# Storing split weights at decode instead of re-splitting them, with ScalarE allowed the q and k copies and a new GpSimd cost in the planner

## The chip, the cores and the metric

One core of one Trainium2 chip runs the kernel. The metric is device time in microseconds of that core, a median of several runs. TensorE is called PE in the profile, VectorE DVE, ScalarE ACT, GpSimd POOL, SyncE SP. Every DMA of this kernel is issued from SP's queue, which is worked off in order.

## The reference, cut to what matters

```python
# q, k, v: [4, 8, 576, 64], f: [4, 8, 576]
scores = q @ k^T / 8 + cum[i] - cum[j]          # cum: running sum of log f; causal
attn = softmax(scores); x = (attn @ v) as [2304, 512]
x = ((x @ w_a) * (x @ w_b)) @ w_out              # first layer, d_ff = 1536
xn = x / rms(x) * rms_g
out = (silu(xn @ w_gate) * (xn @ w_val)) @ w_out2  # second layer
```

Weights arrive as float64 bit patterns. A weight is decoded to float32 and then split into a high part (float32r) and a low part, so that one product becomes three matmuls: high by high, high by low, low by high.

## The kernel before, in words

**Phases.** The 2304 tokens are cut into three chunks of 576, 704 and 1024 tokens. `PHASES` is a list of six (layer m, chunk c): (0,0), (0,1), (1,0), (1,1), (0,2), (1,2), called phases 0 to 5 here. In the trace phase 0 ends at about 235 us, phase 1 at 400, phase 2 at 555, phase 3 at 715. Phases 0 and 2 (`plan_plain`) multiply plainly. Phases 1, 3, 4 and 5 (`plan_wino`) use seven products in place of eight. Attention of the four batches is woven into phases 0 to 3.

**Weights.** An f-tile is 128 of the 1536 inner columns; there are 12 in a layer (FT), taken in thirds of four (QF). Each f-tile has two granules j = 2f and 2f+1 (w_a and w_b, or gate and value), and each third four granules of w_out. In phases 0 and 2 `decode` makes every granule once: SP loads `raw` (512 KB, a ring of two tiles), ACT rebases (L775), DVE shifts (L779) and joins (L783), ACT rounds to the high part (L1646), POOL subtracts for the low part (L791). The result is a `w` tile (512 KB, a ring of seven). A w_out granule is stored split (`wd`, 512 KB, L796); an input granule is stored unsplit (`wf`, 256 KB, L810).

**Re-splitting.** Phases 1 and 3 call `sums` for every f-tile. It loads both unsplit granules (L738), calls `again` for each, which splits them once more (ACT L750, DVE or POOL L753) and stores the split halves to `wd` (L824: 512 KB of the granule "one", 256 KB of "two"). Then it adds and subtracts quarters (L839, DVE or POOL), splits the two combined tiles (ACT L847, DVE or POOL L850) and stores them (`ws`). Phases 4 and 5 load `wd` and `ws` only (L1213). Phase 0 also calls `again` for granules whose second token half comes later.

**Attention.** For three batches `head` copies q twice and k twice per head, rounding them (L1922, on POOL alone), and DVE subtracts for the low parts (L1925).

**Order of the work.** The program is planned ahead: `Plan.op` records each operation with its engine or a tuple of allowed engines, a cost in ns and a priority; `Plan.run` is a list schedule that starts the operation that can start first and, for a tuple, takes the engine that would end it first; `Plan.order` tries nine priority offsets for each 30 us. The costs (`act`, `dve`, `pool1`, `pool2` and so on) are all that it knows of the chip. POOL and DVE operations marked `port` are never planned at one time. Each engine's order is then fixed, so any cost that changes can change the order everywhere.

Of the kernel before, what the change touches and what calls it, by code (L numbers as in the profile page):

```python
# [13 lines left out]
AF = mybir.ActivationFunctionType  # L14
ALU = mybir.AluOpType
# [5 lines left out]
KT, FT = DM // 128, DFF // 128  # L21
# [9 lines left out]
PE, ACT, DVE, POOL, SP = "PE", "ACT", "DVE", "POOL", "SP"  # L31
# [20 lines left out]
    (((3, ALL, 0),), ((2, 0.1, 1.0, 0.7), (3, 0.1, 0.88, 0.3)), 20000),  # L52
]
NG = 2 * FT + 3 * KT

LOADS, SEL = (0, 2, 4, 8), 4

# [38 lines left out]
def act(n, psum=False):  # L96
    return (51 if psum else 93) + n / 1.2
# [6 lines left out]
def dve2(n):  # L104
    return 67 + n / 1.92
# [4 lines left out]


def pool1(n):
    return 55 + n / 0.96


def pool2(n):
    return 75 + 2.25 * n


def half(c, s):  # L120
# [263 lines left out]
class Kernel:  # L384
# [219 lines left out]
    def blocks(self, p):  # L604

        m, c = PHASES[p]
        n = range(len(CHUNKS[c][1]))
        if c == 0:
            if p:
                return [x for q in range(THIRDS) for x in self.plain_blocks(q, n)]  # L610
            ab = lambda fs, ss: [("ab", j, s) for f in fs for j in (2 * f, 2 * f + 1) for s in ss]
            y = lambda q, ss: [("y", i, q, s) for i in range(KT) for s in ss]
            cut = QF + ALONE
            return [
                *self.plain_blocks(0, [0]), *ab(range(QF, cut), [0]), *ab(range(cut, 2 * QF), n),
                *ab(range(QF, cut), [1]), *y(1, n), *self.plain_blocks(2, n), *self.plain_blocks(0, [1]),
            ]
        ahead = int(self.adjoins(p))
        out = [*((x, f) for f in range(2) for x in ("P1", "P2")), ("P7", 0)] if ahead else [("P1", 0), ("P7", 0), ("P2", 0)]
        for f in range(FT):  # L620
            out += [("P6", f), ("P4", f)]
            nxt = [[(x, f + 1)] if f + 1 < FT and (x == "P7" or f >= ahead) else [] for x in ("P1", "P7", "P2")]
            out += [*nxt[0], ("P5", f), *nxt[1], *nxt[2], ("P3", f)]
            if f == FT - 1 or (p < SWAP_AT and f % QF == QF - 1):
                out += [("y", i, f // QF, s) for i in range(KT) for s in n]
            elif p >= SWAP_AT and f and f % QF == FAST_AFTER:
                out += [("z", i, f // QF - 1, k) for k in range(len(FAST)) for i in range(KT // 2)]
        if self.adjoins(p + 1):
            out[-2 * KT :] = [("y", i, THIRDS - 1, s) for s in n for i in range(KT)]
        return out  # L630
# [86 lines left out]
    def weights(self, m, j, t, start=0):  # L717
# [13 lines left out]
        )  # L731
        return w

    def words_of(self, m, j, prio):

        x = self.tile([128, 2, 256], "w32", W32_BUFS, I32, pool=self.dec)
        self.op(
            SP, 420, lambda *_: self.nc.sync.dma_start(self.row(x).bitcast(F32), self.wf[m][j]), reads=[("wf", m, j)],  # L738
            writes=[(x, k) for k in range(2)], prio=prio, nbytes=262144,
        )  # L740
        return x
# [17 lines left out]
    def decode(self, m, js, t, start=0):  # L759

        nc, op = self.nc, self.op
        for j in js:
# [29 lines left out]
                    out=w.tile[:, :, 1, :], in0=i32.tile.bitcast(F32), in1=w.tile[:, :, 0, :].bitcast(F32), op=ALU.subtract  # L792
                )

            def save(j=j, w=w):
                nc.sync.dma_start(self.wd[m][j], self.flat(w.tile))  # L796

            op(SP, 420, load, writes=[raw], prio=t - 14000, nbytes=524288, start=start)
            both = [(i32, k) for k in range(2)]
# [3 lines left out]
            duo = DUO if t < 0 else (ACT,)  # L803
            op(duo, (act(512), dve2(512))[: len(duo)], high, reads=both, writes=[(w, 0)], prio=t - 6000, port=True)
            op(POOL, pool2(512), low, reads=[*both, (w, 0)], writes=[(w, 1)], prio=t - 5500)
            if j >= 2 * FT:
                op(SP, 420, save, reads=[(w, 0), (w, 1)], writes=[("wd", m, j)], prio=t - 4000, nbytes=524288)
            else:
                op(
                    SP, 420, lambda *_, j=j, x=i32: nc.sync.dma_start(self.wf[m][j], self.row(x).bitcast(F32)), reads=both,  # L810
                    writes=[("wf", m, j)], prio=t - 3500, nbytes=262144,
                )
            self.fresh[m, j] = w

    def sums(self, m, f, t):
# [2 lines left out]
        js = (2 * f + 1, 2 * f) if m else (2 * f, 2 * f + 1)  # L818
        one, two = words = [self.words_of(m, j, t - 24000) for j in js]
        whole = []  # L820
        for a, (j, x) in enumerate(zip(js, words)):
            y = self.again(m, j, x, t, a, -3000)
            op(
                SP, 420, lambda y=y, j=j, o=512 * a: nc.sync.dma_start(self.wd[m][j][:, o:], self.flat(y.tile)[:, o:]),  # L824
                reads=[(y, 0), (y, 1)], writes=[("wd", m, j)], prio=t, nbytes=512 * (1024 - 512 * a),
            )
            whole.append(y)
# [357 lines left out]
    def plan_wino(self, p, m, c):  # L1185
# [12 lines left out]
        def load(kind, f, t):  # L1198
            if (kind, f) in loaded:
                return loaded[kind, f]  # L1200
            make = p in SUMS_IN
            if make:
                for x, y in zip((0, 1, "one", "two"), self.sums(m, f, t)):
                    loaded[x, f] = y
                return loaded[kind, f]
            y = self.w_tile()
            if kind in ("one", "two"):
                j = 2 * f + ((kind == "one") == (m == 1))
                key, src, cut = ("wd", m, j), self.wd[m][j], 512 if kind == "two" else 0
            else:  # L1210
                key, src, cut = ("ws", m, f, kind), self.ws[m][f][kind], 0
            op(
                SP, 420, lambda z: nc.sync.dma_start(self.flat(z)[:, cut:], src[:, cut:]),  # L1213
                reads=[key], writes=[(y, 0), (y, 1)], prio=t - 9000, nbytes=512 * (1024 - cut),
            )
            loaded[kind, f] = y
            return y
# [382 lines left out]
    def plan_boot(self):  # L1600
# [12 lines left out]
            self.first_pair(i, FIRST[i % 2], t0 + BOOT_STEP * i)  # L1613
        boot = list(self.plan.nodes)
        self.rows_out(ROWS_AT)
        self.decode(0, (0, 1), t0 + EARLY_AT, EARLY_START)
        self.swapped = self.op(None, 0, self.swap, writes=["late"], after=boot, prio=0)

    def first_loads(self, t):
# [30 lines left out]
    def first_pair(self, i, u, t):  # L1650
# [49 lines left out]
        def each(fn, eng, cost, reads, writes, dt, port=False):  # L1700
            for g in range(2):
                op(eng, cost, partial(fn, g), reads=reads(g), writes=writes(g), prio=t + dt + 100 * g, port=port)
# [9 lines left out]
            writes=both, prio=t + 1900,  # L1712
        )
        op(DVE, 76, lambda *_: nc.vector.reciprocal(out=sm.tile, in_=sm.tile), writes=both, prio=t + 2000)
        each(norm, TRIO, (act(e) + 93, dve2(e) + 62, pool2(e) + 270), of(sm), of(p), 2200, port=True)
        ps, pv = (self.bank(*x) for x in ((("s", S_BANKS) if i % 2 else ("tp", TP_BANKS),) * 2))
        each(transpose, PE, turn_cost(nkb, n), of(p), of(ps), 3500)
        m = 2 * nkb * n
# [193 lines left out]
    def head(self, g, q0, k1, t, sf, b, qk, vr, v):  # L1912
# [5 lines left out]
        if sf:  # L1918
            return [pair], own, values

        def copy(out, x):
            nc.gpsimd.tensor_scalar(out=out, in0=x, scalar1=1.0, scalar2=0.0, op0=ALU.mult, op1=ALU.add)  # L1922

        def rest(out, x, high):
            nc.vector.tensor_tensor(out=out, in0=x, in1=high.bitcast(F32), op=ALU.subtract)  # L1925
# [2 lines left out]
        q, k = (qk, g, 0), (qk, g, 1)  # L1928
        qa, ka = (self.tile([128, S], x + "a", 2, F32R, pool=self.att) for x in "qk")
        n = k1 - q0  # L1930
        op(POOL, pool1(n), lambda x: copy(x[0:64, q0:k1], qr()[:, q0:k1]), reads=[q], writes=[(qa, 0)], prio=t - 9000)
        op(POOL, pool1(n), lambda: copy(b.tile[0:64, g, 0, q0:k1], qr()[:, q0:k1]), reads=[q], writes=[(b, g, 0, 0)], prio=t - 8000)
        op(
            DVE, dve(n), lambda: rest(qa.tile[64:128, q0:k1], qr()[:, q0:k1], qa.tile[0:64, q0:k1]),
            reads=[q, (qa, 0)], writes=[(qa, 1)], prio=t - 7000, port=True,
        )
        op(POOL, pool1(k1), lambda x: copy(x[0:64, :k1], kr()[:, :k1]), reads=[k], writes=[(ka, 0)], prio=t - 7000)
        op(POOL, pool1(k1), lambda: copy(ka.tile[64:128, :k1], kr()[:, :k1]), reads=[k], writes=[(ka, 1)], prio=t - 6000)
        op(
            DVE, dve(k1), lambda: rest(b.tile[0:64, g, 1, :k1], kr()[:, :k1], ka.tile[64:128, :k1]),  # L1940
            reads=[k, (ka, 1)], writes=[(b, g, 1, 0)], prio=t - 5000, port=True,
# [214 lines left out]
```

## Time and profile before

| | |
|---|---|
| median of 3 runs | 1071.0 us (1070.7 to 1071.8) |
| profiled execution, its own time | 1069.92 us |
| its span, first to last instruction | 1068.1 us |
| PE busy | 1041.4 us (98%) |
| DVE, ACT, POOL busy | 845.6, 590.4, 277.2 us |
| moved by DMA | 217.33 MB, mean 203 GB/s |

The span is 1.8 us under the execution's own time, and the execution 1.1 us under the median. Matmuls overlap in the pipeline and their ends are modelled, so that 98% busy says that PE was seldom idle, and not that it ran at its peak.

### The profile page before, as it was taken

To read this page: it belongs to the slowest core of one execution; us is meant where nothing else is said; L and a number is where in the kernel's file an instruction comes from. 1 tells how busy PE (TensorE), PEld (TensorE's weight loads), DVE (VectorE), ACT (ScalarE), POOL (GpSimd) and SP (SyncE) were. 2 spreads that over 40 slices of the span, in tenths; PEclk is the share of its full clock that TensorE was granted. 3 is DMA by queue.
4 is the path that set the end of the run, shared out by engine and by line. 5 is a ranking of instruction groups with operands and counts; after the bars stand their busy time and mean duration, and the time that the engine had idled before them with its cause. 6 is when DMAs were issued, how large, how long until landed. Compare 5 with 4: busy or idle time off the path is not lost.

```text
span 1068.1 us, 19135 instructions
## 1 busy us (share of the span) xinstructions
PE 1041.4 (98%) x6716; PEld 932.8 (87%) x6716; DVE 845.6 (79%) x1893; ACT 590.4 (55%) x1292; POOL 277.2 (26%) x299
## 2 busy tenths in 40 slices
PE   9899999999999999999999999999999999999998
PEld 7678899899999999999989999988888887788886
DVE  7888777799498978988889688866567469979974
ACT  8787766757463766765666664613333254444330
POOL 3444455411222344536341011110000023212000
PEclk9999999999999999999999999999999999999999
DMA  7887465879476845666769576686453634546332
GB/s 195 247 264 242 145 222 169 251 249 346 146 268 210 322 143 153 207 196 215 218 233 331 192 265 258 250 285 198 140 170 123 205 120 148 173 138 182 120 122 79
DMA packets 84848, 217.33 MB, mean 203 GB/s; under 512 B 12320, under 2 KB 22768, under 8 KB 84752
## 3 DMA queue, kind: packets, MB, share of 16 engines
q1 hardware_dynamic: 84752, 216.11, 61.9%
q8 instruction: 53, 0.87, 0.3%
q14 instruction: 43, 0.35, 0.1%
HBM read 141.32 MB, written 74.74 MB: 202 GB/s over the span
## 4 chain that ended last, share of the span: by engine, by line
PE 69%; DVE 13%; DMA 7%; ACT 6%; issue 2%; POOL 2%; SPq 0%; ACTq 0%; DVEq 0%; POOLq 0%
PE m L932 16%; PE m L934 16%; PE m L933 16%; PE s L933 2%; PE s L934 2%; PE s L932 2%; PE s L1954 2%; DMA raw<-wo 2%; PE tp L933 2%; PE tp L934 2%; PE tp L932 2%; PE tp L1595 2%; DVE w L783 2%; PE tp L2018 2%; ACT P L1554 1%
## 5 line engine op out<-in xcount | busy, mean ns | idle before, releaser
L932 PE MATMUL m<-E,w 128*128 128x512 f32 (+3 forms) x672 | 232.8, 346 | 2.5 <-DVE xc L1409 1.3
L934 PE MATMUL m<-E,w 128*128 128x512 f32 (+3 forms) x672 | 228.5, 340 | 2.6 <-DVE w L850 2.3
L933 PE MATMUL m<-E,w 128*128 128x512 f32 (+3 forms) x624 | 213.5, 342 | 0.0
L1321 ACT ACTIVATE a<-m 128x352 f32<-128x352 f32 (+1 forms) x144 | 74.9, 526 | 133.0 <-PE m L934 132.3
L791 POOL TENSOR_TENSOR w<-w,w 128x512 fp32r<-128x512 f32 x72 | 99.5, 1388 | 171.9 <-ACT w L1646 150.8
L932 PEld LDWEIGHTS m<-E,w 128*128 128x128 f32 x672 | 127.3, 189 | 16.8 <-issue 1.8
L933 PE MATMUL m<-Eb,w 128*128 128x352 f32 (+3 forms) x432 | 140.9, 326 | 0.0
L934 PEld LDWEIGHTS m<-E,w 128*128 128x128 f32 x672 | 127.1, 189 | 14.1 <-DVE w L850 2.9
L932 PE MATMUL m<-Eb,w 128*128 128x352 f32 (+3 forms) x384 | 127.7, 333 | 2.0 <-DVE a L1330 2.0
L1330 DVE TENSOR_TENSOR a<-m,a 128x352 f32<-128x352 f32 (+1 forms) x144 | 86.0, 602 | 53.4 <-PE m L934 49.7
L933 PEld LDWEIGHTS m<-E,w 128*128 128x128 f32 x624 | 118.3, 190 | 10.8 <-issue 0.2
L934 PE MATMUL m<-Eb,w 128*128 128x352 f32 (+3 forms) x384 | 126.7, 330 | 0.0
L932 PE MATMUL m<-G,w 128*128 128x352 f32 (+2 forms) x352 | 111.8, 318 | 0.2 <-DVE a L1330 0.2
L933 PE MATMUL m<-G,w 128*128 128x352 f32 (+2 forms) x352 | 108.5, 308 | 1.8 <-DVE G L1460 1.8
L934 PE MATMUL m<-G,w 128*128 128x352 f32 (+2 forms) x352 | 108.4, 308 | 0.0
L1554 ACT ACTIVATE P<-P,mn 128x512 f32<-128x512 f32 (+4 forms) x128 | 76.2, 598 | 16.0 <-DVE mn L1547 15.3
L933 PEld LDWEIGHTS m<-Eb,w 128*128 128x128 f32 x432 | 81.3, 188 | 4.2
L932 PEld LDWEIGHTS m<-Eb,w 128*128 128x128 f32 x384 | 72.1, 188 | 7.9 <-DVE a L1330 2.7
L934 PEld LDWEIGHTS m<-Eb,w 128*128 128x128 f32 x384 | 72.2, 188 | 4.2
L933 PEld LDWEIGHTS m<-G,w 128*128 128x128 f32 x352 | 66.3, 188 | 2.9 <-DVE G L1460 2.2
L932 PEld LDWEIGHTS m<-G,w 128*128 128x128 f32 x352 | 66.4, 189 | 1.8 <-DVE a L1330 0.5
L1547 DVE CUSTOM_DVE_ANT_0 P<-s,mask 128x512 f32<-128x512 f32 (+4 forms) x128 | 61.6, 495 | 7.2 <-PE s L1954 4.0
(271 smaller groups left out, 2337.8 us busy)
## 6 DMA issues: line engine op xcount, KB each, us to landing
w<-wd SPq DMA_DIRECT2D x52, 512.0 KB
wd<-w SPq DMA_DIRECT2D x48, 512.0 KB
ws<-w SPq DMA_DIRECT2D x48, 512.0 KB
w<-ws SPq DMA_DIRECT2D x48, 512.0 KB
w<-wf SPq DMA_DIRECT2D x60, 256.0 KB
wf<-w SPq DMA_DIRECT2D x48, 256.0 KB
raw<-wo SPq DMA_DIRECT2D x24, 512.0 KB
G<-wd SPq DMA_DIRECT2D x18, 512.0 KB
```

The source lines that it names most:

```text
L783: nc.vector.scalar_tensor_tensor(out=x, in0=words(I32, 0), scalar=29, in1=x, op0=ALU.logical_shift_right, op1=ALU.bitwise_or)
L791: nc.gpsimd.tensor_tensor(out=w.tile[:, :, 1, :], in0=i32.tile.bitcast(F32), in1=w.tile[:, :, 0, :].bitcast(F32), op=ALU.subtract)
L932: mm_(o, wh, xh, start=start, stop=False)
L933: mm_(o, wh, xl, start=False, stop=False)
L934: mm_(o, wl, xh, start=False, stop=stop)
L1321: nc.scalar.activation(z[:, :h], bank_.tile[:, :h], AF.Copy)
L1330: nc.vector.tensor_tensor(out=z, in0=bank_.tile[:, :h], in1=z, op=ALU.add)
L1547: nc.vector.tensor_tensor_reduce(out=p.tile[:n, i * w : i * w + w], in0=s[i].tile[:n, :w], in1=masks[i][:n], scale=-0.125, scalar=mn.tile[ ...
L1554: nc.scalar.activation(o, o, AF.Exp, bias=mn.tile[:n, len(s) - 1 : len(s)], scale=-1.0, accum_out=sm.tile[:n, g : g + 1])
L1595: nc.tensor.transpose(ps.tile[:w, c : c + n], p.tile[:n, i * 128 : i * 128 + w], self.ident[:n, :n])
L1954: self.nc.tensor.matmul(x[:n, :e], q.tile[:, a:e], k.tile[:, :e], start=j == 0, stop=j == len(pairs) - 1)
L2018: nc.tensor.matmul(x[64 * g : 64 * g + 64, o : o + n], tiles[g][2][0].tile[:k, i, :], y.tile[:k, to : to + n], start=i == 0, stop=i == blo ...
```

## The change

Input granules get their split form stored when they are decoded, whole for "one" and the second half for "two", except the last third of layer 0 (`ANEW`, f-tiles 8 to 11), for which everything stays as it was. `wf` is stored as before. In `sums` the calls of `again` and the `wd` stores are left only for those four f-tiles; for the other 20 (8 of layer 0, 12 of layer 1) the tiles "one" and "two" are loaded from `wd` in phases 1 and 3, as in phases 4 and 5. Phase 0 takes the last third first and the first third last. The four q and k copies may run on ACT or POOL. The planner takes `pool1` as 80 ns and `pool2` as 30 ns longer; the norm step of the first pairs is corrected by 30 ns, so that its sum stays.

```diff
+ANEW = (FT - QF, FT)
...
 def pool1(n):
-    return 55 + n / 0.96
+    return 135 + n / 0.96
...
 def pool2(n):
-    return 75 + 2.25 * n
+    return 105 + 2.25 * n
...
-                *self.plain_blocks(0, [0]), *ab(range(QF, cut), [0]), *ab(range(cut, 2 * QF), n),
-                *ab(range(QF, cut), [1]), *y(1, n), *self.plain_blocks(2, n), *self.plain_blocks(0, [1]),
+                *self.plain_blocks(2, [0]), *ab(range(QF, cut), [0]), *ab(range(cut, 2 * QF), n),
+                *ab(range(QF, cut), [1]), *y(1, n), *self.plain_blocks(0, n), *self.plain_blocks(2, [1]),
...
+    @staticmethod
+    def anew(m, f):
+        return m == 0 and ANEW[0] <= f < ANEW[1]
...
-            def save(j=j, w=w):
-                nc.sync.dma_start(self.wd[m][j], self.flat(w.tile))
+            o = 512 * (j < 2 * FT and j % 2 != m)
+
+            def save(j=j, w=w, o=o):
+                nc.sync.dma_start(self.wd[m][j][:, o:], self.flat(w.tile)[:, o:])
...
-            if j >= 2 * FT:
-                op(SP, 420, save, reads=[(w, 0), (w, 1)], writes=[("wd", m, j)], prio=t - 4000, nbytes=524288)
-            else:
+            if j >= 2 * FT or not self.anew(m, j // 2):
+                op(SP, 420, save, reads=[(w, 0), (w, 1)], writes=[("wd", m, j)], prio=t - 4000, nbytes=512 * (1024 - o))
+            if j < 2 * FT:
                 op(
...
-        for a, (j, x) in enumerate(zip(js, words)):
+        for a, (j, x) in enumerate(zip(js, words) if self.anew(m, f) else ()):
             y = self.again(m, j, x, t, a, -3000)
...
-            if make:
+            if make and (kind in (0, 1) or self.anew(m, f)):
                 for x, y in zip((0, 1, "one", "two"), self.sums(m, f, t)):
...
-        self.decode(0, (0, 1), t0 + EARLY_AT, EARLY_START)
+        self.decode(0, (2 * (FT - QF), 2 * (FT - QF) + 1), t0 + EARLY_AT, EARLY_START)
...
-        each(norm, TRIO, (act(e) + 93, dve2(e) + 62, pool2(e) + 270), of(sm), of(p), 2200, port=True)
+        each(norm, TRIO, (act(e) + 93, dve2(e) + 62, pool2(e) + 240), of(sm), of(p), 2200, port=True)
...
-        op(POOL, pool1(n), lambda x: copy(x[0:64, q0:k1], qr()[:, q0:k1]), reads=[q], writes=[(qa, 0)], prio=t - 9000)
+        op((ACT, POOL), (act(n), pool1(n)), lambda by, x: copy(by, x[0:64, q0:k1], qr()[:, q0:k1]), reads=[q], writes=[(qa, 0)], prio=t - 9000)
```

The other three copies change in the same way; on ACT a copy is an activation of the kind Copy.

## Rows read from the trace of the kernel before

**Rows 1.** The page's head and section 1: busy us, share, instructions.

```profile
span 1068.1 us, 19135 instructions
...
PE 1041.4 (98%) x6716; PEld 932.8 (87%) x6716; DVE 845.6 (79%) x1893; ACT 590.4 (55%) x1292; POOL 277.2 (26%) x299
```

**Rows 2.** Windows by stage, with their head line.

```profile
core 0: us, PE busy (x) PEld busy (x) DVE busy (x) ACT busy (x) POOL busy (x), PEclk, DMA share, GB/s
0.00:60.00 60.00, 54.48 (x396) 41.77 (x397) 48.78 (x168) 48.90 (x127) 24.32 (x32) 0.97 0.79 217
60.00:235.00 175.00, 169.06 (x1424) 155.24 (x1422) 141.59 (x384) 124.21 (x311) 79.16 (x99) 1.00 0.71 222
235.00:400.00 165.00, 163.24 (x1135) 160.03 (x1136) 135.81 (x340) 97.27 (x228) 44.06 (x54) 1.00 0.68 239
400.00:555.00 155.00, 150.90 (x1258) 144.73 (x1257) 133.94 (x344) 103.58 (x244) 71.69 (x65) 1.00 0.67 204
555.00:715.00 160.00, 156.25 (x999) 150.02 (x998) 123.11 (x263) 86.64 (x186) 18.30 (x24) 0.99 0.71 259
715.00:1069.00 354.00, 347.50 (x1513) 281.01 (x1512) 262.38 (x399) 129.85 (x199) 39.67 (x27) 1.00 0.47 149
```

**Rows 3.** PE's waits: us in total, times, longest; four of 21 rows.

```profile
PE s L1954 <- DVE mn L1547: 2.7, 5, 1.2
PE m L934 <- DVE w L850: 2.3, 1, 2.3
...
PE m L933 <- DVE G L1460: 1.8, 2, 1.6
...
PE s L1978 <- DVE b L1925: 1.0, 2, 0.6
```

**Rows 4.** Windows, all engines: the start of phase 3.

```profile
557.50:560.10 2.60, 0.31 (x2) 0.02 (x1) 1.59 (x4) 0.97 (x3) 1.86 (x3) 1.00 0.05 16
560.80:564.20 3.40, 3.40 (x15) 3.15 (x14) 3.28 (x7) 1.87 (x4) 0.00 (x0) 0.50 0.90 287
```

**Rows 5.** Timeline of ACT there: start, us, instruction, idle before.

```profile
557.21 0.92 ACT L750 ACTIVATE w<-w 128x512 fp32r<-128x512 f32 x2
558.03 0.44 ACT L1321 ACTIVATE a<-m 128x352 f32<-128x352 f32 x1
```

**Rows 6.** Timeline of DVE there.

```profile
558.51 0.53 DVE L1330 TENSOR_TENSOR a<-m,a 128x352 f32<-128x352 f32 x1 [3.06 <-ACT a L1321]
558.95 0.58 DVE L1568 TENSOR_SCALAR sm<-sm 128x2 f32<-128x2 f32 x1
559.42 0.68 DVE L850 TENSOR_TENSOR w<-w,w 128x512 fp32r<-128x512 f32 x1
...
561.09 1.02 DVE L753 TENSOR_TENSOR w<-w,w 128x512 fp32r<-128x512 f32 x2
```

**Rows 7.** Timeline of POOL there.

```profile
551.72 0.74 POOL L839 TENSOR_TENSOR w<-w,w 128x256 f32<-128x256 f32 x1 [3.01 <-DVE w L839]
...
555.90 0.73 POOL L839 TENSOR_TENSOR w<-w 128x256 f32<-128x256 f32 x1
...
557.34 2.16 POOL L1922 TENSOR_SCALAR ka<-qk 64x576 fp32r<-64x576 f32 x3
```

**Rows 8.** Instructions of line 1568: duration ns min/median/max.

```profile
L1568 DVE TENSOR_SCALAR sm<-sm x72: 142/164/1255, 25.7 to 625.1; 128x2 f32<-128x2 f32 x56, 128x1 f32<-128x1 f32 x16
```

**Rows 9.** Timeline of DVE at the end of phase 0.

```profile
235.29 0.48 DVE L1460 TENSOR_TENSOR G<-a,G 128x320 fp32r<-128x320 f32 x1
```

**Rows 10.** Windows of line 1922 alone, 0 to 715 us: the sum.

```profile
sum 715.00, POOL 82.63; mean POOL 16.53
```

**Rows 11.** Timeline of SP: loads of one raw tile, two cycles apart.

```profile
487.46 0.33 SPq L772 DMA_DIRECT2D raw<-wo  x1
...
502.72 0.33 SPq L772 DMA_DIRECT2D raw<-wv  x1
```

**Rows 12.** Windows of line 775 alone, phase 2.

```profile
400.00:555.00 155.00, 18.84 (x28) 1.00 0.67 204
```

More of the change, by code (lines that the diff above doesn't have):

```diff
@@ L1919, in head, with copy @@
             return [pair], own, values
-        def copy(out, x):
-            nc.gpsimd.tensor_scalar(out=out, in0=x, scalar1=1.0, scalar2=0.0, op0=ALU.mult, op1=ALU.add)
+        def copy(by, out, x):
+            if by == ACT:
+                nc.scalar.activation(out, x, AF.Copy)
+            else:
+                nc.gpsimd.tensor_scalar(out=out, in0=x, scalar1=1.0, scalar2=0.0, op0=ALU.mult, op1=ALU.add)
         def rest(out, x, high):
@@ L1930, in head @@
         n = k1 - q0
-        op(POOL, pool1(n), lambda x: copy(x[0:64, q0:k1], qr()[:, q0:k1]), reads=[q], writes=[(qa, 0)], prio=t - 9000)
-        op(POOL, pool1(n), lambda: copy(b.tile[0:64, g, 0, q0:k1], qr()[:, q0:k1]), reads=[q], writes=[(b, g, 0, 0)], prio=t - 8000)
+        op((ACT, POOL), (act(n), pool1(n)), lambda by, x: copy(by, x[0:64, q0:k1], qr()[:, q0:k1]), reads=[q], writes=[(qa, 0)], prio=t - 9000)
+        op((ACT, POOL), (act(n), pool1(n)), lambda by, *_: copy(by, b.tile[0:64, g, 0, q0:k1], qr()[:, q0:k1]), reads=[q], writes=[(b, g, 0, 0)], prio=t - 8000)
         op(
@@ L1936, in head @@
         )
-        op(POOL, pool1(k1), lambda x: copy(x[0:64, :k1], kr()[:, :k1]), reads=[k], writes=[(ka, 0)], prio=t - 7000)
-        op(POOL, pool1(k1), lambda: copy(ka.tile[64:128, :k1], kr()[:, :k1]), reads=[k], writes=[(ka, 1)], prio=t - 6000)
+        op((ACT, POOL), (act(k1), pool1(k1)), lambda by, x: copy(by, x[0:64, :k1], kr()[:, :k1]), reads=[k], writes=[(ka, 0)], prio=t - 7000)
+        op((ACT, POOL), (act(k1), pool1(k1)), lambda by, *_: copy(by, ka.tile[64:128, :k1], kr()[:, :k1]), reads=[k], writes=[(ka, 1)], prio=t - 6000)
         op(
```

## The prediction

> **What bounds the kernel now.** I read the page's engine line first: PE is busy 1041.4 of 1068.1 us [rows 1]. The change removes no matmul, so it can win only what lies between those two numbers, plus what PE loses while nominally busy. Next come the windows by stage [rows 2]: PE's idle time (length less busy) is 5.5 us before 60, 5.9 to 235, 1.8 to 400, 4.1 to 555, 3.8 to 715, and 5.6 of the 353.1 us left to the end. Phases 4 and 5 are untouched, so 21.1 us of idle are in reach at the very most. The other engines are 77 to 86% (DVE) and 54 to 71% (ACT) busy in the four middle stages: busy enough that a late instruction in their fixed order is felt, not so busy that their sums bound anything. Third come PE's waits, which are many and small [rows 3]. One stands out: 2.3 us for line 850, the low half of a combined tile made by `sums`. No row of that list names a DMA, so weights arrive in time today.
>
> That wait is the start of phase 3 [rows 4]: from 557.5 to 560.1 PE works 0.31 us and DMA stands nearly still. Soon after, from 560.8 to 564.2, the granted clock is 0.50, which is 1.2 GHz in place of 2.4. Those 3.4 us do the work of 1.7. So this one hole costs about 2.3 + 1.7 = 4.0 us, the largest single piece that the change can touch.
>
> How it arises is read from three timelines. On POOL the quarter steps of `sums` begin at 551.72 and the third starts at 555.90, 4.18 us later, although one takes 0.74; the time between goes to q and k copies that stand between them in POOL's order [rows 7]. On ACT two calls of `again` for the next f-tile take 0.92 us just before line 1321 [rows 5]. On DVE line 850 stands behind line 1330, which had waited 3.06 us for that line 1321 [rows 6].
>
> **The change part by part.**
>
> *Re-splitting gone.* Of 24 f-tiles 20 lose two ACT calls (0.92 us the pair [rows 5]) and two DVE or POOL calls (1.02 us the pair [rows 6]): 18 us of ACT and 20 us of DVE in all, off PE's path except where a stage starts. At phase 3's start the pair ahead of line 1321 goes, which brings lines 1321, 1330 and 850 forward by 0.8 us (558.03 less 557.21), and a pair ahead of the first quarter step goes too, about 1.0 us by the same durations. That is 1.8 of 2.3. The quarter steps could save more, 4.18 − 2 × 0.74 = 2.7 us, if the copies between them leave POOL. Once the hole is short the slow stretch behind it should go as well. I take −4.0. Bounds: −4.0 (all) and 0 (the hole stays or moves).
>
> At the end of phase 0 PE waits 1.6 us once for line 1460 [rows 3], which runs at 235.29 on DVE [rows 9] after the first `sums` of phase 1 and the combinations of its input. A pair of 1.02 us less in front: I take −1.0, bounds −1.6 and 0.
>
> *Copies on ACT or POOL.* They are 82.6 us of POOL [rows 10]. ACT is planned as shorter, but is busier, so I let half move: 41 us more on ACT, which is busy 374 us in the four stages before 555 [rows 2], so +11%. PE's waits behind these copies are 1.0 us in the row of line 1925 [rows 3]; its waits on ACT should grow in the measure of ACT's load, which on the few us of such waits is some tenths. I take −0.5, bounds −1.2 and +0.8.
>
> One row shows what a copy does to DVE beyond its own chain: line 1568, two columns wide, takes 0.58 us at 558.95 while POOL runs three copies up to 559.50 [rows 6, 7], against a median of 0.164 and a longest of 1.255 [rows 8]. The Trainium skill (SBUF — State Buffer, "SBUF: two separate sides") says that VectorE and GpSimd share one pair of ports as an exclusive lock, held for the whole instruction, and that ScalarE has its own. By that rule each copy moved frees DVE for all of its time, and the term would be up to the 2.7 us of PE's waits on line 1547 larger, −3.2 in place of −0.5. The row agrees with the lock; it does not show that PE waited for it.
>
> *Stores at decode.* Each f-tile stores 512 + 256 KB, 0.786 MB. 8 of them in phase 0 add 6.3 MB, 12 in phase 2 add 9.4 MB; the same bytes leave phases 1 and 3. Phase 2 goes from 204 to 265 GB/s and by proportion from 0.67 to 0.87 of the DMA engines' time; phase 0 (60 to 235) from 0.71 to 0.83 [rows 2]. What is late next is `raw`: with two tiles, the next load waits for the join of the one before the last. One tile's loads at 487.46 and 502.72 are two cycles apart [rows 11], 7.6 us a cycle, 3.8 us a granule. The stage needs 28 granules in 155 us [rows 12], 5.5 us each, attention included. At 204/0.67 = 305 GB/s one further 512 KB ahead of a load costs 1.7 us, 0.86 us a granule: 4.7, still under 5.5. Where no attention is between, PE takes a granule in about the ring's own time, and there the delay counts. I count 8 stored granules in each of phases 0 and 2 so, hence the upper bound 16 × 0.86 = 13.8 us; lower bound 0. Seven `w` tiles lie between decode and PE, so I stay near the lower end, +1.5.
>
> The Trainium skill speaks against this part: DMA: Bandwidth & Descriptors, "Latency and other measured facts", gives HBM's access latency as 0.2 us on average and 2 us at high load. By it each load would take up to 1.8 us longer, and the same 16 granules would cost 16 × 0.9 = 14 us, an estimate from that page. No run here shows the latency by itself.
>
> *Loads in phases 1 and 3.* 20 f-tiles load 0.786 MB each from `wd`, 15.7 MB, as much as the stores that left. Phases 4 and 5 load the same tiles with no DMA in PE's waits. I take 0. Upper bound: one hole like phase 3's 2.35 us at each of two starts, +4.7. A gain is excluded, since nothing waits for these tiles now.
>
> *Order of thirds, early decode, longer GpSimd costs.* The blocks are the same in number and size; the last third, decoded in the crowded first 72 us, is the one that stores nothing new. 0, but the whole list is ordered anew: ±2 us, as large as the single waits that such an order makes or removes [rows 3].
>
> Sum: −4.0 − 1.0 − 0.5 + 1.5 + 0 = −4.0 us. Against the profiled execution's 1069.9 that is 1065.9; it stands 1.1 under the median, so the median goes from 1071.0 to **1067.0 us**.
>
> **The rivals.**
> *The waits move (about 1071).* The hole at phase 3's start closes, but another opens elsewhere, or the first `wd` load is late there: −4.0 − 1.0 − 0.5 + 1.5 + 4.7 = +0.7, 1071.7. For it: none of PE's 21 rows of waits comes from a shortage, all come from order. Against: ACT and DVE have 18 and 20 us less to do in the order.
> *The stores hold decode back (slower).* Place: `raw` in phase 2 and the middle of phase 0. Price: 13.8 against gains of 5.5, +8.3, 1079; with half caught by the `w` ring 13.8/2 − 5.5 = +1.4, 1072.4. It decides once each stored granule costs over 5.5/16 = 0.34 us. For it: DMA at 0.87. Against: 4.7 under 5.5.
> *A better order everywhere (faster).* The planner's GpSimd times were short; with them right and copies off POOL, half of the 5.9 and 4.1 us idle of phases 0 and 2 goes, 5 us more: 1062.
> *The change does nothing* is part of the first rival: if planner and rings absorb all, ±2.
>
> **How the numbers follow.** Forecast 0.48, with a range of its own of 1063 to 1068.8; waits move 0.20; stores bite 0.20; better order 0.12. Two measurements of this kernel are told apart from about 0.2%, 2.1 us. Faster: 0.48 + 0.12 = 0.60. Same: the waits that move, 0.20. Slower: the stores, 0.20. The range reaches from the better order, 1061, to the nearer half of the stores, 1075; outside stay about 0.05 below and 0.1 above.
>
> **What would show it.** The longest wait of PE in phase 3's start is under 1 us and no half-clock stretch follows (else the −4.0 fails). Line 750 has 20 calls, not 60; bytes moved rise from 217 to 233 MB. Phase 2 shows about 265 GB/s; a cycle of `raw` stays under 9.3 us, and PE's waits name no weight from line 791 (else the stores bite). L1922's copies show on ACT about as often as on POOL. The prediction is wrong if PE's idle time in phases 0 and 2 together grows by more than 5 us, or if phases 1 and 3 show PE waiting for DMA.

## The result, and the profile after

The kernel after takes 1058.25 us (1057.13 to 1059.58, 4 runs), the kernel before in the same comparison 1071.4. The ratio is 0.9877, 95% interval [0.986, 0.9894]: 13 us faster, three times the forecast 4, and below the range. The profiled execution took 1057.13 us, its span is 1055.4.

The page's head and engine line answer to [rows 1]. The other rows are from its sections on DMA.

```profile
span 1055.4 us, 19131 instructions
...
PE 1036.5 (98%) x6716; PEld 931.0 (88%) x6716; DVE 830.3 (79%) x1877; ACT 605.6 (57%) x1324; POOL 193.2 (18%) x203
...
DMA packets 90607, 233.05 MB, mean 221 GB/s; under 512 B 12960, under 2 KB 23408, under 8 KB 90512
...
w<-wd SPq DMA_DIRECT2D x72, 512.0 KB
...
w<-wd SPq DMA_DIRECT2D x44, 256.0 KB
```

PE does the same 6716 matmuls. Its idle time, span less busy, falls from 1068.1 − 1041.4 = 26.7 to 18.9 us, and its busy time by 4.9 us. POOL loses 84 us of work, ACT gains 15, DVE loses 15, and 15.7 MB more are moved.

For the stages I divided both kernels where PE begins the blocks of a new phase. First the windows of before, for the three phases that matter, divided so:

```profile
60.00:237.60 177.60, 170.83 (x1436) 157.01 (x1435) 144.19 (x392) 125.65 (x315) 79.16 (x99) 1.00 0.71 223
...
390.40:555.30 164.90, 160.80 (x1331) 154.45 (x1330) 142.30 (x365) 110.38 (x261) 77.61 (x74) 1.00 0.65 200
555.30:702.10 146.80, 143.05 (x940) 139.20 (x939) 117.59 (x254) 83.30 (x180) 17.25 (x22) 0.99 0.69 253
```

And the windows of after, columns as in [rows 2]:

```profile
0.00:60.00 60.00, 54.76 (x414) 42.04 (x415) 50.04 (x173) 48.97 (x126) 20.83 (x28) 0.97 0.77 217
60.00:233.20 173.20, 168.26 (x1417) 156.22 (x1416) 145.13 (x392) 140.59 (x353) 53.53 (x58) 1.00 0.81 263
233.20:383.00 149.80, 148.99 (x1017) 145.84 (x1016) 115.52 (x285) 83.50 (x193) 28.43 (x35) 1.00 0.73 254
383.00:549.50 166.50, 164.07 (x1370) 157.49 (x1370) 140.98 (x375) 126.56 (x293) 64.44 (x60) 1.00 0.79 260
549.50:690.70 141.20, 140.05 (x940) 137.66 (x939) 109.15 (x232) 72.88 (x158) 11.69 (x14) 1.00 0.73 259
690.70:1056.00 365.30, 360.33 (x1570) 291.70 (x1568) 269.52 (x424) 133.13 (x204) 14.24 (x11) 1.00 0.48 155
```

PE's idle time, length less busy, falls by 6.8 − 4.9 = 1.8 us in phase 0, by 4.1 − 2.4 = 1.7 in phase 2 and by 3.8 − 1.2 = 2.6 in phase 3. Phase 3's part was forecast; phases 0 and 2, where the copies and the decoding are, were not. The DMA shares of 0.81 and 0.79 at 263 and 260 GB/s are those that the prediction worked out (0.83 and 0.87 at 265), a little lower.

PE's waits after, nine of 19 rows, the longest first, columns as in [rows 3]:

```profile
PE tp L1603 <- ACT P L1586: 2.1, 3, 1.1
PE s L1965 <- DVE mn L1555: 2.0, 5, 0.7
PE tp L1603 <- ACT w L781: 1.6, 1, 1.6
PE m L940 <- ACT a L1329: 1.2, 2, 0.7
PE tp L2029 <- ACT pt L2076: 1.2, 3, 0.5
PE warm L1616 <- DVE ones L430: 1.1, 1, 1.1
PE tp L1603 <- ACT pt L2076: 0.9, 3, 0.4
PE m L940 <- DMA w<-wd: 0.6, 2, 0.4
...
PE m L942 <- POOL w L797: 0.5, 1, 0.5
```

Lines 850 and 1460, the 2.3 and 1.8 us of [rows 3], have left the list (they are 858 and 1468 here). The list sums to 14.6 us against 22.2 in 21 rows before; the waits on DVE alone fall from 17.2 to 5.1, those on ACT rise from 4.5 to 7.9. The last two rows shown are new: waits for a stored tile at the start of phase 1 and for a decoded low half (L797, which is L791 before).

The windows at phase 3's start answer to [rows 4]:

```profile
549.50:552.10 2.60, 2.60 (x19) 2.60 (x18) 2.57 (x6) 2.38 (x6) 1.17 (x2) 1.00 1.05 409
552.10:555.50 3.40, 3.40 (x23) 3.40 (x22) 3.15 (x7) 1.97 (x5) 0.74 (x1) 1.00 1.03 385
```

PE works without a gap and keeps its full clock, where before it worked 0.31 of 2.60 us and then ran at 0.50 for 3.4 us [rows 4].

Last, the line of `again` and the windows of the copies alone (up to 691 us, ACT's line and then POOL's):

```profile
L756 ACT ACTIVATE w<-w x20: 407/618/635, 111.9 to 348.4; 128x512 fp32r<-128x512 f32 x16, 128x256 fp32r<-128x256 f32 x4
```

```profile
0.00:691.00 691.00, 37.17 (x70) 1.00 0.77 256
```

```profile
0.00:691.00 691.00, 35.91 (x58) 1.00 0.77 256
```

`again` runs 20 times, and 70 of the 128 copies went to ACT, about half, both as predicted.

### The profile page after: what moved, and what is told of

Same layout as the page of the kernel before. It is cut to its first block, busy times and chain, and to the rows that moved or that the text cites. A ratio compares the mean times of both kernels' runs of the same rounds, so it can differ in the third digit from the quotient of the medians.

```text
span 1055.4 us, 19131 instructions
## 1 busy us (share of the span) xinstructions
PE 1036.5 (98%) x6716; PEld 931.0 (88%) x6716; DVE 830.3 (79%) x1877; ACT 605.6 (57%) x1324; POOL 193.2 (18%) x203
## 4 chain that ended last, share of the span: by engine, by line
PE 62%; DVE 13%; ACT 9%; DMA 8%; issue 6%; POOL 2%; SPq 0%; DVEq 0%; POOLq 0%; ACTq 0%
PE m L940 15%; PE m L942 14%; PE m L941 14%; PE s L941 2%; PE s L942 2%; PE s L940 2%; ACT P L1562 2%; PE tp L941 2%; PE tp L942 2%; PE tp L940 2%; DMA raw<-wv 2%; DVE w L789 2%; DMA w<-wd 1%; PE tp L2029 1%; PE tp L1603 1%
## 5 line engine op out<-in xcount | busy, mean ns | idle before, releaser
L797 POOL TENSOR_TENSOR w<-w,w 128x512 fp32r<-128x512 f32 x72 | 97.1, 1354 | 201.7 <-ACT w L1654 161.3
L941 PEld LDWEIGHTS m<-E,w 128*128 128x128 f32 x624 | 118.2, 189 | 10.8
L1465 ACT ACTIVATE G<-a 128x352 fp32r<-128x352 f32 (+3 forms) x100 | 47.1, 473 | 46.1 <-DVE a L1451 17.8
L940 PEld LDWEIGHTS m<-G,w 128*128 128x128 f32 x352 | 66.2, 188 | 2.9 <-issue 1.7
```

What stands on the lines that cost most here:

```text
L797: nc.gpsimd.tensor_tensor(out=w.tile[:, :, 1, :], in0=i32.tile.bitcast(F32), in1=w.tile[:, :, 0, :].bitcast(F32), op=ALU.subtract)
L940: mm_(o, wh, xh, start=start, stop=False)
L941: mm_(o, wh, xl, start=False, stop=False)
L1465: nc.scalar.activation(out(0), x(), AF.Copy)
```

## The experiments

Two theories stood at first. By the first the gain is the re-splitting that went: its two holes were most of the forecast. By the second it is the copies that left POOL. A third came up at once: the planner writes every order anew, so a part may win or lose only because its list came out well.

**One part at a time, and the order shaken without any part.** Each is the kernel before with one part of the diff; the fourth changes one planner cost by 1 ns, so that only the order differs.

```diff
 e1_stores_alone: the lines of decode, sums and the order of thirds, nothing else
 e2_copies_alone: the four copies on (ACT, POOL), nothing else
 e3_costs_alone: pool1 55 -> 135, pool2 75 -> 105, norm 270 -> 240
 e4_order_shaken:
-    return 69 + n / 0.96
+    return 70 + n / 0.96
```

> The kernel before with the stores at decode and the order of thirds alone; q and k copies on GpSimd only, GpSimd costs as before. Theory A (re-splitting gone is the gain): at least 8 of the 13 us, 1063 or less, with phases 1 and 3 shorter. Theory B (copies or the GpSimd costs are the gain): within 3 us of before, 1068 to 1073, or slower where the stores delay the raw loads. Theory C (any new order of the list gives some us either way): anything between 1063 and 1076.

> The kernel before with the q and k copies allowed on ScalarE or GpSimd, nothing else. Theory A: within 3 us of before. Theory B, copies: phases 0 to 3 lose the waits behind GpSimd, 1064 or less, and the hole of 2.3 us at the start of phase 3 closes although both calls of the second split are still there. Theory C: 1066 to 1076, with no relation to what was moved.

> The kernel before with the planner's longer GpSimd times alone; the same operations on the same engines or nearly so. Theory A: within 3 us of before. Theory B, costs: 1066 or less, since waits on GpSimd that the plan did not foresee go. Theory C: 1066 to 1076.

> The kernel before with one cost of the planner 1 ns longer (VectorE's fixed part, 70 in place of 69 ns), so the work is the same and only its order may differ. Theory C (a new order is worth some us by itself): moves by over 3 us, up or down. Theories A and B: within 2 us of before.

Measured: stores alone 0.9945 [0.9925, 0.9966], copies alone 0.9871 [0.9846, 0.9896], costs alone 0.9956 [0.9939, 0.9973], order shaken 0.9974 [0.9958, 0.9991]. The copies alone give as much as the whole change, 13 us or more. But the costs, which take no work away and only reorder it, with 27 of POOL's 299 instructions put on DVE and ACT, "give" 4.7, and a shaken order 2.8, so no single ratio can be read to better than some 0.4%.

**One part left out, and the orders of both shaken.** The next runs take one part out of the change, or shake the orders of the copies, of the change and once more of before (69 to 71).

```diff
 e5_without_copies: the change, all four copies on POOL
 e6_without_stores: the change, without the new stores, with `again` for all f-tiles
 e14_stores_and_copies: the change, pool1, pool2 and norm as before
 e7_copies_shaken (copies alone), e13_change_shaken (the change):
-    return 69 + n / 0.96
+    return 70 + n / 0.96
 e18_order_shaken_again (the kernel before):
-    return 69 + n / 0.96
+    return 71 + n / 0.96
```

> The changed kernel with the q and k copies put back on GpSimd alone: stores and GpSimd costs stay. Theory B (the copies off GpSimd carry the change): most of the gain is gone, 0.993 to 0.998 of before. Theory A (stores and costs carry it together): 0.990 or less. Theory C (each new order is some us by luck): no better than a guess, 0.985 to 1.000.

> The changed kernel with the stores and the order of thirds taken back: copies on ScalarE or GpSimd and the longer GpSimd costs alone. Theory B: as good as the whole change or as the copies alone, 0.985 to 0.990. Theory A (the stores give some us more): 0.991 or more. Theory C: 0.985 to 1.000.

> The changed kernel with the planner's old GpSimd costs. With copies on either engine every kernel so far stands at 0.987 to 0.994; if the costs are worth nothing of their own, this one stands there too, and the stores' part cannot be told from the scatter of orders. If the costs are needed with the stores, 0.995 or more.

> The copies alone on the kernel before, with one VectorE cost of the planner 1 ns longer. Theory B: 0.985 to 0.990, as the copies alone in the first order. Theory C (that 0.987 was a lucky order): falls back to 0.993 or more.

> The changed kernel with one VectorE cost of the planner 1 ns longer. If the change's 0.988 is what its parts are worth, 0.985 to 0.991. If it is a lucky order, it goes to the level of the copies shaken, 0.991 to 0.995.

> The kernel before with DVE's planner cost 69 made 71, nothing else. If the kernels with all q and k copies on GpSimd scatter as those measured so far (0.9945 to 1.0018, mean 0.998), it lies there again, 1066 to 1074 us. If a gain of over 0.7% can come from an order alone, without copies, it can lie below 0.993.

Together with the first runs this makes 13 kernels with the same rings. The table has the ratio to before; the mean clock of TensorE over the runs; the mean time multiplied by that clock, which is an estimate of what the kernel would take had no stretch run at half clock (before was measured in five comparisons: its mean times lie from 1071.5 to 1073.1 us, this product only from 1065.5 to 1066.2); and from the one profiled execution of each PE's idle time (span less busy) and the sum of PE's waits on DVE over the rows of its list.

| copies | kernel | ratio, 95% interval | clock | time × clock, us | PE idle, us | waits on DVE, us |
|---|---|---|---|---|---|---|
| POOL | before (95 runs) | 1 | 0.9939 | 1065.9 | 26.7 | 17.2 |
| POOL | e1 stores | 0.9945 [0.9925, 0.9966] | 0.9949 | 1062.0 | 24.6 | 13.5 |
| POOL | e3 costs | 0.9956 [0.9939, 0.9973] | 0.9939 | 1061.9 | 26.0 | 14.2 |
| POOL | e4 shaken | 0.9974 [0.9958, 0.9991] | 0.9954 | 1065.3 | 25.4 | 15.1 |
| POOL | e5 stores, costs | 1.0018 [0.9998, 1.0038] | 0.9917 | 1064.2 | 25.1 | 15.9 |
| POOL | e18 shaken | 0.9971 [0.9941, 1.0] | 0.9929 | 1061.9 | 23.4 | 10.8 |
| either | after | 0.9877 [0.986, 0.9894] | 0.9983 | 1056.5 | 18.9 | 5.1 |
| either | e2 copies | 0.9871 [0.9846, 0.9896] | 0.9950 | 1054.1 | 17.1 | 8.2 |
| either | e6 copies, costs | 0.9941 [0.9913, 0.9969] | 0.9946 | 1057.9 | 20.1 | 9.3 |
| either | e7 copies, shaken | 0.9929 [0.9906, 0.9953] | 0.9968 | 1058.8 | 20.7 | 10.0 |
| ACT | e12 copies | 0.9941 [0.9923, 0.9958] | 0.9934 | 1058.7 | 20.7 | 10.7 |
| either | e13 all, shaken | 0.9938 [0.9911, 0.9964] | 0.9946 | 1058.5 | 20.3 | 8.5 |
| either | e14 stores, copies | 0.9950 [0.9932, 0.9967] | 0.9954 | 1061.5 | 21.1 | 9.6 |

With the copies on POOL alone the means of the last three columns are 1063.5, 25.2 and 14.5 us; with the copies movable they are 1058.0, 19.8 and 8.8. No kernel of one group reaches into the other: 1061.5 stands against 1061.9, 21.1 against 23.4, 10.7 against 10.8. So movable copies are worth about 5.5 us of work (standard error 1.1 from the scatter in the groups), and it shows as 5.4 us less idle time of PE and as 5.7 us less waiting for DVE, though these two come from one execution of each kernel. In the plain ratio the groups' means differ by 0.0056, 6.0 us, and the groups just touch: 0.9950 (e14) against 0.9945 (e1).

Taken one by one, several of these runs missed what was expected of them: e5 lies above all three of its ranges, e6 where the stores would carry some of the gain, e13 at the level named for a lucky order. It is the two groups that carry the argument, not a single run.

The stores are worth nothing in the same table. Among kernels with movable copies those with stores (after, e13, e14) have a mean time × clock of 1058.8, those without 1057.4; with copies on POOL it is 1063.1 (e1, e5) against 1063.8. That is +1.4 and −0.7, in a scatter of 2 us from kernel to kernel. The costs come out at −0.6 and −0.7.

Of the 14.1 us between the means of all runs of before and after (1072.4 and 1058.3), 9.4 are time × clock and the other 4.7 the clock. Of the 9.4, 5.5 are the copies; before stands 2.4 above the mean of its group and after 1.5 below its own, which makes the rest. That part and the clock's I put down to these two orders: shaken once, by 1 ns, the change measures 0.9938.

Which waits are left is seen best in the copies alone. Rows of the list of PE's waits in e2, those on the lines of [rows 3] and on lines 1330 and 1321:

```profile
PE s L1957 <- DVE mn L1547: 2.0, 5, 0.7
...
PE m L933 <- DVE G L1460: 1.3, 1, 1.3
...
PE s L1981 <- DVE b L1928: 1.0, 1, 1.0
...
PE m L932 <- DVE a L1330: 0.7, 2, 0.4
PE m L932 <- ACT a L1321: 0.7, 1, 0.7
```

Line 850 is gone from it, although `again` still runs 60 times there, and PE does not stop at phase 3's start (windows of e2):

```profile
552.50:555.10 2.60, 2.60 (x36) 2.37 (x34) 2.48 (x6) 1.42 (x3) 0.00 (x0) 1.00 0.08 27
```

POOL is idle in that window: no copy stands in its list there. In e5, with `again` gone but the copies on POOL, the hole is still there (waits, and windows at its phase 3's start):

```profile
PE m L940 <- ACT w L855: 1.3, 1, 1.3
...
PE m L942 <- DVE w L858: 0.6, 1, 0.6
```

```profile
561.60:565.00 3.40, 1.83 (x9) 1.55 (x10) 3.40 (x9) 2.45 (x5) 0.00 (x0) 1.00 0.80 274
565.00:568.40 3.40, 3.40 (x13) 3.40 (x13) 3.00 (x8) 1.28 (x3) 0.00 (x0) 0.50 0.91 269
```

So the re-splitting did not have to go for this hole to close. But neither did the copies have to leave POOL: in e1 (no re-splitting in phase 3) PE doesn't stop there, and in e3 (re-splitting) for 0.3 us, with all copies on POOL. The windows of both, the first 12 us of their phase 3, e1 first:

```profile
558.30:570.30 12.00, 12.00 (x77) 11.34 (x75) 8.50 (x18) 6.81 (x16) 7.18 (x10) 1.00 0.99 340
```

```profile
557.20:569.20 12.00, 11.66 (x81) 10.86 (x80) 9.78 (x24) 7.80 (x19) 3.89 (x6) 1.00 0.87 310
```

In those 12 us PE is idle for at most 0.2 us in each of the seven kernels with movable copies; with copies on POOL it is 0 in e1, 0.3 in e3 and 1.0 to 2.4 in the other four. So movable copies go with the closed hole, and yet an order alone can close it: e3 changes nothing but the planner's costs.

At the end of phase 0 the re-splitting counts: the wait for line 1460 is there in seven of the eight kernels of the table that re-split (1.3 us in e2, e6, e7 and e12, 1.6 in before and e4, 2.2 in e3; in e18 PE waits 1.1 for a load instead). All kernels without re-splitting there also have the new order of thirds; in them the wait is gone, or 0.3 (e5), but within some 10 us other waits stand in its place: 0.6 us for loads of stored tiles in after, e13 and e14, and 2.0 and 1.4 in all in e1 and e5. What is left of the gain is about 0.7 to 1.0 us with movable copies and little with the copies on POOL.

**Copies on ACT alone.** Is the gain POOL's absence from the ports that it shares with DVE in the planner's model, so that more is won the fewer copies POOL keeps?

```diff
-        op(POOL, pool1(n), lambda x: copy(...), reads=[q], writes=[(qa, 0)], prio=t - 9000)
+        op((ACT,), (act(n),), lambda by, x: copy(by, ...), reads=[q], writes=[(qa, 0)], prio=t - 9000)
```

> The kernel before with the q and k copies on ScalarE only. If what matters is that GpSimd and its lock on VectorE's port are spared, as good as the copies on either engine or better, 0.985 to 0.991, and the time from rebase to the join's end in phase 0 is 3.5 us or less in place of 4.4. If ScalarE becomes what PE waits for (it is at 71% in phase 0, and gets 41 us more there), 0.995 or more.

Measured 0.9941 [0.9923, 0.9958], between the two ranges, and 1058.7 us of time × clock: inside the group, no better than kernels with half the copies left on POOL. The sign that was named did come: from the rebase to the join's end in phase 0 it takes 3.0 us, against 4.2 in before. But over both layers, where this falls from 4.4 to 3.3, the time from the issue of the raw load to the rebase on ACT rises from 5.6 to 6.6, so most of what the join wins is lost ahead of it. PE's waits show where ACT is late (e12's list):

```profile
PE tp L1595 <- ACT pt L2068: 1.9, 3, 1.0
...
PE s L1981 <- ACT ka L1923: 1.2, 1, 1.2
```

The last row is a copy that PE now waits for, on ACT.

How a copy on POOL costs PE time is not shown by these runs. Three ways are open. First, a copy can lengthen what DVE does beside it. In before's trace, worked out from starts and ends, the shift of line 779 takes 0.66 us as a mean of the 10 that overlap a copy and 0.42 of the 46 that overlap nothing on POOL; the maxima of line 1547 (128x512) take 0.68 to 0.69 in both cases. Over the 89 DVE instructions that overlap a copy (those with at least five like them beside an idle POOL) this lengthening sums to 8.5 us, in e2 to 5.8, in e12 to 0. That agrees in sign, but from before to e2 it falls by 2.7 us where PE's waits on DVE fall by 9.0; it is 8.7 in e7 and 5.1 in e5, which stand in the wrong groups for it. Second, DVE can wait for the copy that its subtraction reads: 6.8 us of DVE's idle time in before, but only 0.4 in e1 and 1.1 in e3, which are no faster for it. Third, the planner never puts a POOL operation and a DVE operation marked `port` at one time, so each copy that leaves POOL frees places for DVE in the plan, whatever the chip does. No run took that rule out of the planner, so this rival is untested.

**The new stores twice.** The stores hid well; how far from harm are they? Each new store is issued a second time, to a tensor that nothing reads, 15.7 MB more.

```diff
+            def twice(j=j, w=w, o=o):
+                nc.sync.dma_start(self.wx[m][j][:, o:], self.flat(w.tile)[:, o:])
...
+                if j < 2 * FT:
+                    op(SP, 420, twice, reads=[(w, 0), (w, 1)], writes=[("wx", m, j)], prio=t - 3900, nbytes=512 * (1024 - o))
```

> The changed kernel with every new store of an input granule issued a second time, to a place that nobody reads: 15.7 MB more written in phases 0 and 2. If the stores were priced rightly in the prediction (1.5 us for the first set, up to 13.8 where they hold the raw loads back), it is 2 to 10 us slower than the changed kernel, 0.990 to 0.997 of before. If stores at this rate are hidden altogether, it stays within 2 us of it, 0.986 to 0.990.

Measured 1078.33 us, 1.008 [1.0062, 1.0099], slower than either range: 20 us over after, and 1074.6 − 1058.8 = 16 us of time × clock over the mean of the three other kernels with stores and copies. The page's DMA line, then the windows of phases 0 and 2 and two of PE's waits:

```profile
DMA packets 96368, 248.79 MB, mean 231 GB/s; under 512 B 13600, under 2 KB 24048, under 8 KB 96272
```

```profile
60.00:245.00 185.00, 175.41 (x1421) 159.26 (x1421) 145.21 (x406) 142.98 (x353) 52.97 (x58) 0.99 0.86 280
...
398.00:570.00 172.00, 166.02 (x1385) 158.97 (x1384) 150.04 (x401) 128.18 (x295) 57.72 (x50) 1.00 0.83 279
```

```profile
PE s L1971 <- DVE mn L1561: 5.5, 10, 0.9
PE tp L1609 <- ACT P L1592: 3.7, 3, 2.4
```

PE's idle time in these two phases is 9.6 and 6.0 us, against 4.9 and 2.4 in after, at DMA shares of 0.86 and 0.83 against 0.81 and 0.79. Over the span it grows by 11.3 us (1076.4 − 1046.2 = 30.2 against 18.9); the other 9.7 us of the longer span are busy time of PE with the same 6716 matmuls, and stay open. The longest of PE's waits are for attention's maxima and probabilities on DVE and ACT, not for weights. That these come late because the steps of decoding stand late ahead of them in those engines' order is argued, not shown. From SP's issue of a raw tile (L772 in before, L778 in after, L779 here) to the rebase on ACT (L775, L781, L782) it takes, as a mean over 68 of the 72 granules (the first two of each layer left out), worked out from the starts in the timelines, 5.60 us before, 6.12 after and 7.47 here. The second set of stores costs a granule 1.35 us. Of the first 0.5 only a part is the stores': e2, which has none of them, stands at 5.95, and e1, which has them alone, at 5.94.

**A third raw tile.** From these cycles I formed a theory that the ring of two raw tiles paces phases 0 and 2, and that the copies win by giving it back sooner: from the rebase to the end of the join it takes 4.44 us before, 3.69 with the copies alone. By it a third raw tile should win as much as the copies and add nothing to them. The space for it is taken from the `w` ring, six tiles in place of seven, so each has a control with six.

```diff
 e9_raw3_before, e17_raw3_shaken (and 69 -> 70), e11_raw3_changed, e16_copies_raw3:
-W_BUFS, W32_BUFS, A_BUFS, BP_BUFS = 7, 4, 7, 4
+W_BUFS, W32_BUFS, A_BUFS, BP_BUFS = 6, 4, 7, 4
-P_BUFS, PT_BUFS, RAW_BUFS = 5, 4, 2
+P_BUFS, PT_BUFS, RAW_BUFS = 5, 4, 3
 e10_w6_before, e15_w6_changed: the first pair of lines alone
```

> The kernel before with three raw tiles in place of two; the space is taken from the w ring, six tiles in place of seven. If the two raw tiles set the pace of phases 0 and 2 (issue to join 10 us a cycle, 5 us a granule), a third lets a cycle take half as long again, and the kernel is at least 6 us faster than its control with six w tiles and two raw tiles, perhaps faster than before. If not, the two are within 3 us of each other.

> The control: the kernel before with six w tiles in place of seven and two raw tiles. Same or slower than before, up to 10 us, since a finished weight must be used sooner.

> The changed kernel with three raw tiles and six w tiles. If the raw ring still paces phases 0 and 2 there, where a load takes 6.5 us to its rebase in place of 5.6, faster than the changed kernel: 0.980 to 0.986 of before. If the change has taken the ring off the path, 0.987 or more, worse by what the missing w tile costs.

> The control of three raw tiles on the changed kernel: six w tiles and two raw tiles. If the missing w tile is what cost the changed kernel its gain (stored weights hold a w tile until the store has landed, and phases 1 and 3 load two more tiles each), this one is as slow as the one with three raw tiles, 0.994 to 1.000. If the third raw tile itself does harm there, it stays at 0.988 to 0.991.

> The kernel before with the copies on either engine, three raw tiles and six w tiles; no stores, old costs. Copies and third raw tile shorten the same cycle. If the cycle was the limit and is one no more, they do not add: 0.984 to 0.990. If they add, 0.980 or less.

> The kernel before with three raw tiles and six w tiles as in the run e9, and DVE's planner cost 69 made 70, so that the list comes out in another order. If the ring of raw tiles paces the phases of projections, most of the gain of e9 (0.9873) stays: 0.985 to 0.992, some 1056 to 1064 us. If e9 was a lucky order, it falls back to its control with six w tiles (0.9964): 0.994 to 1.002. Between 0.992 and 0.994 it tells nothing.

| | ratio, 95% interval | clock | time × clock, us |
|---|---|---|---|
| e10 before, six w | 0.9964 [0.9945, 0.9984] | 0.9967 | 1064.8 |
| e9 before, three raw | 0.9873 [0.9855, 0.989] | 1.0000 | 1057.8 |
| e17 before, three raw, shaken | 0.9954 [0.9932, 0.9976] | 0.9954 | 1062.0 |
| e15 after, six w | 0.9926 [0.9901, 0.9952] | 0.9983 | 1061.8 |
| e11 after, three raw | 0.9956 [0.993, 0.9982] | 0.9937 | 1061.0 |
| e16 copies, three raw | 0.9942 [0.9922, 0.9963] | 0.9950 | 1061.2 |

The first run spoke for the ring, 0.9873 against 0.9964. The shaken run takes most of that back: 0.9954, which its expectation had named as the sign of a lucky order. Beside the copies a third raw tile gives nothing (1061.2). So no gain of the ring is shown, but it isn't excluded either: e9 and e17 differ by one order, e9 stands among the kernels with movable copies (1057.8; PE idle 18.8, waits on DVE 9.8) and e17 among those without (1062.0; 23.5 and 13.5), and their mean is 4.9 us under the one control. That is about what the theory asked for; two orders and one control don't settle it.

**Beyond both.** No kernel beats the change by more than the scatter; the copies alone (0.9871) are as good with 15.7 MB less traffic.

## Why the prediction was wrong, step by step

**The step that failed is the term for the copies**: "I take −0.5, bounds −1.2 and +0.8". They are worth about −5.5 us, by the means of the two groups. I priced them by the single row of PE's waits that names their consumer, 1.0 us of line 1925 [rows 3], and by ACT's added load. But most of PE's list, 17.2 of 22.2 us, is waits on DVE under many other lines, and I left these out of the term. With movable copies they fall by 5.7 us in the mean, spread over maxima, sums, combined inputs and products. That movable copies bring this is shown by the two groups; how they do it is not, as said above. One row had pointed to it, the 0.58 us of line 1568 [rows 6, 8].

By the rule of the Trainium skill quoted there (SBUF — State Buffer, "SBUF: two separate sides") the term was −3.2, the nearer of the two. The same section names the lock only for VectorE instructions in a two-port mode or with two inputs in SBUF, so "frees DVE for all of its time" read too much into it. The trace agrees in sign (0.66 against 0.42 us for the shift), but not that the wait on maxima carries it: line 1547 takes 0.68 to 0.69 us with or without a copy beside it, and its row falls from 2.7 to only 2.0 us in e2. And that rule alone would have made e12, with no copy on POOL, the best of its group, which it isn't.

This term alone, −5.5 for −0.5, would have given 1062.0, still inside the stated range. What took the time below it is, as far as these runs show, the luck of one order: 3.9 of the 9.4 us of time × clock are not the copies', and 4.7 us more are clock.

**Re-splitting gone, −4.0 and −1.0.** The hole at phase 3's start closed with its half-clock stretch, as forecast, but the credit was wrong: e2 closes it with all calls of `again`, e5 leaves it open without them. The copies between the quarter steps on POOL [rows 7], which that paragraph took as an addition, are the likelier cause, but e1 and e3 close it with all copies on POOL. It was also not the only wait that "stands out". A second, left out of [rows 3], is its twin: PE waits 2.2 us once for line 1571 (attention's sums), up to 36.5 us, and runs at half clock from 38.6 (wait, then windows of before):

```profile
PE s L1954 <- DVE sm L1571: 2.2, 1, 2.2
```

```profile
34.00:36.50 2.50, 0.29 (x3) 0.08 (x2) 2.47 (x8) 1.39 (x4) 1.27 (x1) 1.00 0.68 127
...
38.60:42.00 3.40, 3.40 (x16) 3.24 (x16) 2.84 (x9) 2.37 (x7) 2.78 (x3) 0.50 0.86 239
```

No copy runs on POOL there. This wait is gone from after's list too, though PE's idle time before 60 us is nearly the same (5.5 and 5.2). The −1.0 at the end of phase 0 was right in cause and in size for after, 1.6 us of wait becoming 0.6, but the 0.6 is a wait for the new loads.

**Stores at decode, +1.5.** Together with the re-splitting that they replace, the stores come to +1.4 and −0.7 us; the sum of both terms was −3.5, so the two cancel, and that sum failed too. How it divides between them is not known. The forecast of slower loads came true in part: from issue to rebase a granule takes 0.2 to 0.6 us longer in a kernel with stores than in one with the same copies without (0.86 was worked out). But the comparison "4.7 under 5.5" was not what kept them hidden. It took a cycle of 7.6 us from two loads of one stretch [rows 11]; the mean cycle before, issue to end of join, is 10.0, so that 5.0 + 0.86 is over 5.5, and yet the cycle after is 9.6. It also counted 512 KB of the 768 that a pair of granules stores: with all, 1.29 us a granule and 20.6 in place of 13.8, an estimate by the same rate, near the 16 to 20 us that the second set cost.

**Loads in phases 1 and 3, 0.** Nearly right: PE waits 0.6 us, in two waits, for `w` from `wd`, at the start of phase 1.

**Order, ±2.** Too narrow. Two kernels that differ by 1 ns of one cost lie 2.8 us (before), 6.2 (copies alone) and 6.5 (the change) apart; in time × clock it is 0.6, 4.7 and 2.0. Without the luck of this order the change would lie between its group's mean ratio of 0.992 and the 0.994 of e13, some 1063 to 1065 us, inside the range given: that it fell below is luck.

**The rivals.** "A better order everywhere", 1062, was nearest, with idle time in phases 0 and 2 down by 3.5 us where it had 5. Of its two causes the copies off POOL hold, and the truer costs of GpSimd don't: those give −0.6 and −0.7 us. Of the signs named, bytes, shares of DMA, the split of the copies, the 20 calls and the closed hole came true. Three spoke against the forecast by their words: PE waits for DMA in phase 1 (0.6 us), PE waits once for line 791 (0.5 us), and a tile's loads in phase 2 are 10.0 us apart in the mean (from SP's starts), not under 9.3, though they were 9.6 apart before. None of them marks a loss of that size.

## What to carry to other kernels

Work on an engine that is seldom busy can still be what holds the busy ones, on the chip or in the planner's rules: price an engine's relief against all waits on the engines that it excludes or disturbs, here DVE's 17 us, and not by the one wait that names its product. Where a planner writes the order, shake it (1 ns of one cost) several times with and without a part before a gain is given to that part; here one order alone moved 6 us, and a change of costs alone closed a hole that looked like the work of a part. And split such gains into work and granted clock, or a lucky clock is taken for a good idea.

## What the runs showed of the hardware that was not expected

The clock differs from run to run of one kernel. In e18 ten runs span 1062.49 us, at a mean clock of 1.000, to 1075.16, at 0.989. Its profiled execution has a mean of 0.990 (core's line), and one long stretch at half clock early on (window):

```profile
core 0: 1071.0 us, clock 0.990
```

```profile
32.90:53.40 20.50, 20.05 (x89) 11.84 (x89) 13.15 (x44) 13.16 (x30) 7.22 (x9) 0.50 0.53 167
```

The mean clock follows the length of such stretches: 20.5 us in all within e18's span, 6.8 in before's (two of 3.4), 3.4 in after's, none in e9's, whose mean is 1.000. After's one stretch stands right behind a piece in which PE was busy 1.79 of 3.40 us:

```profile
52.00:55.40 3.40, 3.40 (x17) 3.23 (x16) 2.12 (x7) 2.90 (x8) 0.00 (x0) 0.51 0.41 83
48.60:52.00 3.40, 1.79 (x11) 1.08 (x9) 3.34 (x10) 2.57 (x7) 1.27 (x1) 1.00 0.90 296
```

Over the 95 runs of before the time falls by 8.6 us for each 0.01 of mean clock (correlation −0.66), near the 10.7 that 0.01 of the time would be. Why after, e15 and e9 keep more of their clock than the others is open, and so is most of the 4.9 us by which PE's busy time fell: one half-clock stretch less, 3.4 us at half speed, is 1.7 of it.
